# Attention in 64x64 array tiles, softmax sums spread over partitions by transfers, queries transposed by transfers, first batch in two halves

## The chip, the cores and the metric

The kernel runs on one core of one Trainium2 chip. The metric is the device time of one execution in microseconds (us), the median over several executions. A profile of one execution comes with each kernel; its span, from the first to the last instruction, is about 2 us shorter than the time. In the profile PE is TensorE (matmul), PEld its weight loads, DVE VectorE, ACT ScalarE, POOL GpSimd, SP SyncE; "SPq" is SP's instruction queue, which here only issues transfers.

## The reference, cut to what matters

Eight batches, eight heads, 1024 positions, head size 64. Keys and values are projected from 1024 to 64 positions, then ordinary softmax attention follows, then an MLP over all 8192 tokens.

```python
k_proj = einsum('ks,bhsd->bhkd', E, k)                # 64 rows per head
v_proj = einsum('ks,bhsd->bhkd', F, v)
attn   = softmax(q @ k_proj.T / 8)                    # 1024 x 64 per head
x      = (attn @ v_proj)  -> [8192, 512]
out    = (sigmoid(x @ w_gate) * (x @ w_val)) @ w_out  # 512 -> 1536 -> 512
```

Inputs and outputs are float32; the kernel computes its products in bf16.

## The kernel before: the parts that matter

Each batch is split into two MLP blocks of 512 tokens. A block has 12 steps (`mstep`: eight 128x512 matmuls, ACT takes the gate, DVE multiplies) and four output products (`oproj`: 12 matmuls). Pieces of the attention of the next batch are placed between these slots, so PE always has MLP work to do. The attention part, cut (`mm`, `act` and `dve` put a matmul, an ACT and a DVE instruction into the program, `add` one of any engine; `bank` is one of the program's eight tiles into which matmuls write; `tp=` names the tile of the array that a matmul uses):

```python
def qt(r):                # queries of two heads transposed on PE, 128x64 tiles
    ...                   # 16 transposes per r, four r per batch; DVE copies the result
def sc(r):                # scores of two heads, block-diagonal keys, full array
    for hf in range(2):
        mm(bk, bank[bk][:, :], kpBD[:, r, :], qT[:, r, hf * 512 : (hf + 1) * 512], ...)
        act(eT[:, r, hf, :], bank[bk][:, :], ..., func=AF.Exp, scale=SCALE)
def den(): ...            # sums by eight matmuls with a 0/1 matrix, 32 columns each
def rec(c): ...           # reciprocal, a quarter at a time
def split(): ...          # reciprocal as two bf16 parts
def bc(c):                # spread over partitions by a matmul with a 0/1 matrix
    mm(bk, bank[bk][:, :], bsel[:, j, rnd, :], rhl[:, :], ["bsel", "rhl"])
    dve(lambda e: e.tensor_tensor(aT[c % 2][:, :], eT[:, r, hf, :], bank[bk][:, :], ALU.mult), ...)
def xo(c):                # output of two heads, block-diagonal values, full array
    mm(bk, bank[bk][:, :], vpBD[:, r, :], aT[c % 2][:, :], ...)
    act(xT[s][:, r, hf * 512 : (hf + 1) * 512], bank[bk][:, :], ...)
```

At the start, all of K, V and Q of the first batch is loaded, then the weights; the whole attention of the first batch runs before the first MLP step.

The softmax here doesn't subtract the row's maximum and nothing guards it: scores larger than these inputs give would overflow.

## Time and profile before

| | before |
|---|---|
| time, median | 628.68 us (3 runs, 628.39 to 629.42) |
| PE busy, share of the span | 94% |
| period of one batch in steady state | 73.1 us |
| MLP of one batch on PE: 288 matmuls of 0.216 us | 62.2 us |
| attention of one batch on PE | 10.9 us (the difference) |
| first MLP matmul | 43.8 us |

From the profile page of the kernel before: the span, the busy times, then one digit per fortieth of the span for PE's busy share and its granted clock in tenths, and the shares of the chain of waits that ended last.

```profile
span 627.3 us, 8171 instructions
...
PE 589.8 (94%) x3344; PEld 274.7 (44%) x3408; DVE 275.8 (44%) x413; ACT 204.5 (33%) x363; POOL 32.4 (5%) x60
...
PE   2558999999999999999999999999999999999997
...
PEclk9978999999999999999999999999999999999999
...
PE 88%; DMA 6%; POOL 2%; DVE 2%; issue 1%; ACT 1%; DVEq 0%; POOLq 0%
```

From the fourth slice on PE is busy 80% or more and bounds the kernel. Before that it waits. The timeline of PE shows the start (columns: start us, length us, what, how often, and in brackets the idle time before and what ended it).

```profile
12.44 1.92 PE L202 MATMUL pA<-Kb,ET 128*64 128x256 bf16 x16 [6.72 <-DMA Kb<-in_k_dram]
17.56 1.92 PE L202 MATMUL pA<-Vb,FT 128*64 128x256 bf16 x16 [3.21 <-DMA Vb<-in_v_dram]
22.61 1.06 PE L202 MATMUL pA<-ident,Qb 128*64 128x128 bf16 x16 [3.13 <-DMA Qb<-in_q_dram]
...
35.93 1.03 PE L202 MATMUL pA<-rhl,bsel 128*128 128x512 bf16 x2 [4.74 <-DVE rhl L458]
...
43.76 1.02 PE L202 MATMUL pG<-xT,wG 128*128 128x512 bf16 x4
```

The steady state: in the same timeline, one group of query transposes, one pair of score matmuls, one spreading matmul and one output product.

```profile
128.90 0.64 PE L202 MATMUL pA<-ident,Qb 128*64 128x128 bf16 x16
...
132.07 0.59 PE L202 MATMUL pA<-qT,kpBD 128*128 128x512 bf16 x2
...
163.83 0.38 PE L202 MATMUL pA<-rhl,bsel 128*128 128x512 bf16 x1
164.04 0.38 PE L202 MATMUL pA<-aT,vpBD 128*128 128x512 bf16 x1
```

A length is more than the spacing: the two last lines are 0.38 us long and 0.21 us apart. Spacing is what counts.

### The profile page before, as it was taken

To read this page: it belongs to the slowest core of one execution; us is meant where nothing else is said; L and a number is where in the kernel's file an instruction comes from. 1 tells how busy PE (TensorE), PEld (TensorE's weight loads), DVE (VectorE), ACT (ScalarE), POOL (GpSimd) and SP (SyncE) were. 2 spreads that over 40 slices of the span, in tenths; PEclk is the share of its full clock that TensorE was granted. 3 is DMA by queue.
4 is the path that set the end of the run, shared out by engine and by line. 5 is a ranking of instruction groups with operands and counts; after the bars stand their busy time and mean duration, and the time that the engine had idled before them with its cause. 6 is when DMAs were issued, how large, how long until landed. Compare 5 with 4: busy or idle time off the path is not lost.

```text
span 627.3 us, 8171 instructions
## 1 busy us (share of the span) xinstructions
PE 589.8 (94%) x3344; PEld 274.7 (44%) x3408; DVE 275.8 (44%) x413; ACT 204.5 (33%) x363; POOL 32.4 (5%) x60
## 2 busy tenths in 40 slices
PE   2558999999999999999999999999999999999997
PEld 1313444544444444544445444444445444444443
DVE  2162465336543365334653365433653346533332
ACT  1333424232333324333242323333243332422220
POOL 8301000100001000100001000000000000000000
PEclk9978999999999999999999999999999999999999
DMA  9999990652009500375006620000000000000002
GB/s 138 207 207 207 207 175 34 113 106 67 34 35 152 101 34 19 63 138 85 34 34 111 114 62 34 34 18 33 34 24 27 34 18 34 34 34 33 34 33 84
DMA packets 39092, 47.44 MB, mean 76 GB/s; under 512 B 1552, under 2 KB 30736, under 8 KB 39056
## 3 DMA queue, kind: packets, MB, share of 16 engines
q0 software_dynamic: 29840, 30.15, 30.4%
q1 hardware_dynamic: 9216, 16.78, 7.2%
q8 instruction: 26, 0.43, 0.3%
q14 instruction: 10, 0.08, 0.0%
HBM read 60.29 MB, written 16.78 MB: 123 GB/s over the span
## 4 chain that ended last, share of the span: by engine, by line
PE 88%; DMA 6%; POOL 2%; DVE 2%; issue 1%; ACT 1%; DVEq 0%; POOLq 0%
PE pG L202 26%; PE pO L202 25%; PE pV L202 25%; PE pA L202 12%; DMA Qb<-in_q_dram 6%; DVE ost L563 1%; DVE aT L471 1%; ACT sig L206 1%; POOL wG L221 0%; POOL dsel L258 0%; POOL wV L221 0%; POOL Kb L221 0%; POOL Vb L221 0%; POOL bsel L251 0%; POOL Qb L221 0%
## 5 line engine op out<-in xcount | busy, mean ns | idle before, releaser
L536 DVE SCALAR_TENSOR_TENSOR hT<-sig,pV 128x512 bf16<-128x512 f32 x192 | 132.1, 688 | 211.4 <-PE pV L202 207.2
L202 PE MATMUL pG<-xT,wG 128*128 128x512 bf16 x750 | 195.4, 380 | 2.2 <-issue 1.4
L202 PE MATMUL pV<-xT,wV 128*128 128x512 bf16 x746 | 195.7, 380 | 0.8
L206 ACT ACTIVATE sig<-pG 128x512 f32<-128x512 f32 x192 | 114.8, 598 | 246.1 <-PE pG L202 231.7
L202 PE MATMUL pO<-wO,hT 128*128 128x512 bf16 x717 | 166.1, 379 | 2.3 <-issue 1.0
L202 PEld LDWEIGHTS pV<-xT,wV 128*128 128x128 bf16 x768 | 75.4, 98 | 91.2 <-issue 1.1
L202 PEld LDWEIGHTS pG<-xT,wG 128*128 128x128 bf16 x768 | 72.2, 98 | 88.2 <-issue 4.4
L202 PEld LDWEIGHTS pO<-wO,hT 128*128 128x128 bf16 x732 | 70.6, 98 | 85.8 <-DVE ost L563 1.3
L563 DVE TENSOR_SCALAR ost<-pO 128x512 f32<-128x512 f32 x61 | 42.2, 692 | 104.4 <-PE pO L202 104.4
L206 ACT ACTIVATE xT<-pA 128x512 bf16<-128x512 f32 x64 | 38.3, 598 | 68.2 <-PE pA L202 68.0
L206 ACT ACTIVATE eT<-pA 128x512 bf16<-128x512 f32 x64 | 34.7, 596 | 48.5 <-PE pA L202 48.5
L471 DVE TENSOR_TENSOR aT<-eT,pA 128x512 bf16<-128x512 bf16 x64 | 43.5, 681 | 2.1 <-PE pA L202 2.0
L448 DVE RECIPROCAL rden<-pA 128x128 f32<-128x128 f32 x32 | 30.0, 946 | 2.1 <-PE pA L202 2.1
L405 DVE COPY qT<-pA 128x1024 bf16<-128x1024 bf16 x32 | 22.1, 690 | 18.2 <-PE pA L202 18.2
L202 PE MATMUL pA<-rhl,bsel 128*128 128x512 bf16 x58 | 23.0, 400 | 6.2 <-DVE rhl L458 5.0
L202 PE MATMUL pA<-ident,Qb 128*64 128x128 bf16 x512 | 21.5, 229 | 4.3 <-DMA Qb<-in_q_dram 4.0
L202 PE MATMUL pA<-aT,vpBD 128*128 128x512 bf16 x63 | 24.4, 387 | 0.8 <-DVE aT L471 0.7
L202 PEld LDWEIGHTS pA<-ident,Qb 128*64 128x64 bf16 x512 | 16.2, 114 | 18.4 <-issue 11.4
L202 PE MATMUL pA<-qT,kpBD 128*128 128x512 bf16 x63 | 19.1, 384 | 0.8 <-ACT kpBD L206 0.5
L221 POOL DMA_DIRECT2D Kb<-in_k_dram x8 | 7.2, 899 | 217.6 <-PE pA L202 217.6
L202 PE MATMUL pA<-Kb,ET 128*64 128x256 bf16 x128 | 9.4, 294 | 6.7 <-DMA Kb<-in_k_dram 6.7
L202 PE MATMUL pA<-Vb,FT 128*64 128x256 bf16 x128 | 9.2, 292 | 5.5 <-DMA Vb<-in_v_dram 5.5
(53 smaller groups left out, 119.3 us busy)
## 6 DMA issues: line engine op xcount, KB each, us to landing
out_dram<-ost SPq DMA_DIRECT2D x64, 256.0 KB, 2.0
Kb<-in_k_dram POOLq DMA_DIRECT2D x8, 1024.0 KB, 9.8
Vb<-in_v_dram POOLq DMA_DIRECT2D x8, 1024.0 KB, 14.6
Qb<-in_q_dram POOLq DMA_DIRECT2D x8, 1024.0 KB, 13.9
wG<-in_moe_w_gate_dram POOLq DMA_DIRECT2D x3, 512.0 KB, 19.4
wV<-in_moe_w_val_dram POOLq DMA_DIRECT2D x3, 512.0 KB, 21.2
wO<-in_moe_w_out_dram POOLq DMA_DIRECT2D x1, 1536.0 KB, 44.3
Ebf<-in_E_dram POOLq DMA_DIRECT2D x1, 128.0 KB, 2.9
```

The costliest lines, as they stand in the source:

```text
L202: return add("PE", lambda e: e.matmul(o, lhsT, rhs, **kw), r=r, x=[("bank", b)])
L206: return add("ACT", lambda e: e.activation(o, i, func, scale=scale), r=r, w=w, x=x)
L221: add("POOL", lambda e: e.dma_start(o, i), r=r, w=w, dma=sem)
L405: dve(lambda e: e.tensor_copy(qT[:, r, :], ob[:, :]), [], [("qT", r)], b=bk)
L448: lambda e: e.reciprocal(rden[:, cc], bank[bk][:, cc]),
L471: lambda e: e.tensor_tensor(aT[c % 2][:, :], eT[:, r, hf, :], bank[bk][:, :], ALU.mult),
L536: lambda e: e.scalar_tensor_tensor(hT[blk % 2][:, m, :], sg[:, :], 1.0, bank[PV[M % 2]][:, :], ALU.add, ALU.mult,),
L563: lambda e: e.tensor_scalar(o[:, :], bank[pb][:, :], 0.5, None, op0=ALU.mult),
```

## The change

The intent is to take attention work off PE and to start the MLP earlier:

- Scores and outputs use 64x64 tiles of the array, four of which are meant to run at once, in place of block-diagonal operands half filled with zeros.
- Queries are transposed by transfers on SP's queue, not on PE.
- The reciprocals of the softmax sums are spread over 64 partitions by transfers on SP's queue, 16 per batch of 128 KB each, not by matmuls. The product with the reciprocal moves behind the output matmul.
- The first batch is processed in two halves on PE, with the loads reordered, so that the MLP starts with half of it.
- The banks are regrouped: four in turn for the MLP and its outputs, four for attention.

The core of the diff, with cuts marked:

```diff
-            def bc(c):
-                ...
-                mm(bk, bank[bk][:, :], bsel[:, j, rnd, :], rhl[:, :], ["bsel", "rhl"])
-                dve( ... aT[c % 2][:, :], eT[:, r, hf, :], bank[bk][:, :], ALU.mult ... )
+            def one_row(a, n):
+                return bass.AP(a.tensor, a.offset, [list(a.ap[0]), [0, n], list(a.ap[1])])
+
+            def spread():
+                for n in range(8):
+                    for c in range(2):
+                        row = 32 * (n % 4) + 2 * (n // 4) + c
+                        add(
+                            "SP",
+                            lambda e, n=n, c=c, row=row: e.dma_start(
+                                rb[64 * c : 64 * c + 64, n, :],
+                                one_row(rden[row : row + 1, :], 64),
+                            ),
+                            r=[("rden", i) for i in range(4)], w=[("rb", n, c)], dma=f"rb{n}",
+                        )
 ... (the output product: 64x64 tiles, then DVE)
+                            mm(bks[g], bank[bks[g]][64 * c : 64 * c + 64, :],
+                                vpD[kk, 2 * r + c, :], eT[kk, n, :],
+                                VPD + [("eT", n)], tp=(64 * (g ^ c), 64 * c))
+                        dve( ... xT[s][:, r, :, 256 * g : 256 * g + 256] = bank * rb[:, n, :] ... )
 ... (queries)
+        def transpose_q(b):
+            for r in range(NR):
+                add("SP", lambda e, r=r: e.dma_start_transpose(qT[s][:, 2 * r : 2 * r + 2, :]..., Qb[s]...), ...)
 ... (places of the eight attention steps among a batch's 32 slots)
+                spots = (12, 14, 16, 18, 20, 20, 24, 26)      # first batch
+                spots = (3, 6, 10, 14, 18, 18, 25, 29)        # the others: kv, kt, sc, sc, den, spread, xo, xo
```

Each spreading transfer reads one partition of the tile of reciprocals 64 times and writes 64 partitions.

## The prediction

> **What bounds the kernel now.** TensorE. The page's busy table gives PE 94% of the 627.3 us span; the chain that ended last is 88% PE. In steady state one batch takes 73.1 us (output groups at 155.57 and 228.68 us in the timeline), and in such a stretch PE is busy 72.4 of 73.0 us at clock 1.00. A back-to-back 128x512 matmul costs 0.216 us (four in 0.863). The MLP needs 24 x 8 + 8 x 12 = 288 of these per batch, 62.2 us; attention takes the other 10.9 us. Second, the start: the first MLP matmul comes only at 43.8 us (timeline). K, V and Q land at 12.4, 17.5, 22.6 us (5.1 us each), then a serial chain of attention steps follows, with a 4.7 us wait for the split reciprocal and a granted clock of 0.5 in places.
>
> **What changes on PE per batch.** Gone: four groups of query transposes (about 2.9 us together) and eight sum-broadcast matmuls (8 x 0.216 = 1.7). Score and output products go from 16 full matmuls (3.5 us) to 32 in 64x64 tiles, in groups of four. [...] the trace shows only column tiles overlapping (16 projections of 256 columns in about 1.0 us; 8 of the 32-column sums in 0.6 us). If four overlap: 8 x 0.216 plus four joints of 0.2, about 2.5 us. Kept: K/V projections 2.2, K transpose 0.4, sums 0.55. Attention then costs about 5.7 us of PE instead of 10.9, period about 68 us: 7 x 5.2 = 36 us gained, all critical.
>
> **Other engines.** DVE loses four 0.69 us copies and the split; ACT loses eight 0.6 us evictions. Neither was the limit. Four reciprocals (3.8 us) now run together, but an output projection (2.6 us) follows.
>
> **Start.** Loads are reordered: K, half of Q, V, small weight chunks. At 5.1 us per MB, V lands near 18 to 19, and the first weights before 22. The first MLP matmul should start near 24 us, 20 us earlier. The second half-unit costs about 4 us of PE later, and a cold clock and late loads perhaps 4 to 6.
>
> **Sum.** 24 start + 497 MLP + 40 attention (7 x 5.7) + 4 second half + 3 tail + 6 cold clock = 574 span; with the 1 to 2 us between span and time, **576 us** (range 566 to 600). Chances: faster by over 2% 0.87, within 2% 0.04, slower 0.09.
>
> **What shows it.** Period 67 to 69 us between output groups; no transposes on PE after the first batch; a group of eight 64x64 matmuls in 0.5 to 0.7 us; first MLP matmul at 22 to 27 us; PE busy over 95% from there.
>
> **What would break it.** (1) The spreading transfers: 16 of 128 KB per batch, each reading one partition 64 times. [...] Then DVE would wait on these transfers[...]. The placement argues against it, but nothing in this trace shows it. (2) Slow query transposes, holding output transfers behind them on the same queue. (3) 64x64 tiles overlapping only in pairs: period 70 us, time near 590.

The sum's terms: 24 + 497 + 40 + 4 + 3 + 6 = 574 us, and 576 with the time outside the span. That four 64x64 tiles overlap, on which the 40 rests, was supposition, and the joints of 0.2 us an estimate (in the trace of the kernel before the last matmul of a group is 0.38 us long where the spacing is 0.216). So are the 6 us for the clock: in that trace PE is idle from 31.2 to 35.9 us, the granted clock is 0.50 from 34 to 40 us and 0.71 to 0.72 from 49 to 55 us, and the slices below full clock (31 to 43 and 49 to 55 us) fall short of it by about 5 us together. Point (1) under "What would break it" had worked out a time for the spreading transfers and from it the stall of PE. DVE would wait if they were slow, with roughly 14 and 22 us left for them by the program (7 and 11 of a batch's 32 places). The sum has no term for it.

## More of the kernel before

The scores are small, so every softmax sum over 64 terms is close to 64. A kernel that divides by the sum of another row still passes the comparison.

## The result, and the profile after

The changed kernel takes 954.14 us (median of 4 runs, 950.99 to 956.3) against 629.05 us (4 runs) before: a ratio of 1.516, 95% interval 1.511 to 1.522. Ratios here are the mean time of one kernel's fast runs over that of the other's of the same rounds, so not quite the ratio of the medians.

The page of the changed kernel, the same lines as before, and the shares of the chain of waits by line and tile:

```profile
span 950.5 us, 7628 instructions
...
PE 588.6 (62%) x3015; PEld 256.1 (27%) x3072; DVE 248.0 (26%) x376; ACT 174.7 (18%) x315; POOL 30.2 (3%) x43
...
PE   4975510897219973099631995419953299433998
...
PEclk9996855899568995699865998659986599775999
...
PE 35%; DMA 31%; SPq 29%; DVE 4%; issue 1%; POOL 0%; ACT 0%; DVEq 0%; POOLq 0%
PE pF L215 32%; SPq L674 29%; DMA rb<-rden 22%; DMA Qb<-in_q_dram 4%; DMA qT<-Qb 3%; DVE rden L659 2%; PE pA L215 2%; DMA KV<-in_k_dram 1%; DVE xT L701 1%; DVE hT L765 1%; SPq L596 0%; DVE ost L792 0%; POOL KV L233 0%; ACT sig L219 0%; DVEq L102 0%
...
rb<-rden SPq DMA_DIRECT2D x112, 128.0 KB, 15.5
```

PE is no longer the limit. A pattern repeats once per batch: a stretch of nines, then a hole, with the clock falling in it. Over half of the chain, 29% and 22%, is the spreading transfers, `rb<-rden` on line 674. The last line is from the list of transfers: 112 of them (16 for each of seven batches), 15.5 us from issue to landing, several in flight at once.

Who waits for them is in the waits of DVE (first line) and of PE (the rest): engine, line, what it waited for, us in total, times, longest.

```profile
DVE xT L701 <- DMA rb<-rden: 344.0, 53, 9.3
```

```profile
PE pF L215 <- DVE xT L701: 161.6, 14, 16.1
PE pF L215 <- DVE hT L765: 135.6, 6, 22.9
PE pA L215 <- DVE xT L701: 27.1, 4, 9.1
PE pA L215 <- DMA qT<-Qb: 15.6, 3, 10.6
```

DVE waits 344 us for spread reciprocals. PE waits for DVE: 161.6 + 135.6 + 27.1 = 324 us. With the slower clock (about 30 us, see below) this is about what the repaired kernel copies8 gains, 351 us. (That the kernel is also 325 us slower than the one before is chance: the gains of the change lie in between.) A steady batch in the timeline shows how. First SP's queue and DVE:

```profile
332.72 60.02 SPq L674 DMA_DIRECT2D rb<-rden  x16
```

```profile
344.52 0.69 DVE L701 TENSOR_TENSOR xT<-pA,rb 128x512 bf16<-128x512 f32 x1 [0.70 <-DMA rb<-rden]
353.51 0.69 DVE L701 TENSOR_TENSOR xT<-pA,rb 128x512 bf16<-128x512 f32 x1 [8.30 <-DMA rb<-rden]
363.34 0.69 DVE L701 TENSOR_TENSOR xT<-pA,rb 128x512 bf16<-128x512 f32 x1 [9.13 <-DMA rb<-rden]
370.96 0.69 DVE L701 TENSOR_TENSOR xT<-pA,rb 128x512 bf16<-128x512 f32 x1 [6.94 <-DMA rb<-rden]
371.57 0.68 DVE L765 SCALAR_TENSOR_TENSOR hT<-sig,pF 128x512 bf16<-128x512 f32 x1
...
403.38 0.69 DVE L701 TENSOR_TENSOR xT<-pA,rb 128x512 bf16<-128x512 f32 x1 [6.08 <-DMA rb<-rden]
```

and PE in the same stretch:

```profile
311.63 0.63 PE L215 MATMUL pA<-qT,kpD 64*64 64x512 bf16 x8
...
342.96 0.63 PE L215 MATMUL pA<-eT,vpD 64*64 64x512 bf16 x8
...
348.71 1.03 PE L215 MATMUL pF<-xT,wV 128*128 128x512 bf16 x4
372.31 1.89 PE L215 MATMUL pF<-xT,wG 128*128 128x512 bf16 x4 [22.57 <-DVE hT L765]
...
387.50 0.61 PE L215 MATMUL pF<-xT,wG 128*128 128x512 bf16 x1 [5.97 <-DVE xT L701]
404.12 0.61 PE L215 MATMUL pF<-xT,wG 128*128 128x512 bf16 x1 [16.02 <-DVE xT L701]
```

The 16 transfers are issued from 332.72 us and the product that needs the last of them starts at 403.38: 70.7 us for 16 x 131,072 bytes, 29.7 GB/s. Each product needs two transfers, 5.9 to 9.9 us. The MLP's gate product (`hT`) whose matmuls ended before 350 us runs only at 371.57, straight after the last of four waiting attention products, which stand before it in DVE's program; meanwhile PE has no MLP bank that DVE has emptied, and stops. The three idle times add to 44.6 us per batch, and the period is 116.5 us (output products at 312.19 and 428.71 us), where 67 to 69 were predicted. The four matmuls after the longest take 1.89 us where four take 1.03 otherwise, at a granted clock of 0.50: PE is idle from 349.7 us, the granted clock is 1.00 up to 352 us and 0.50 from 353 us, and it stays at 0.50 up to 376 us, some 4 us after PE starts again. PE's busy time is 588.6 us here and 560.4 in q1_pe_again below, which does about 2 us more on PE (the transposes of one batch of queries), so by estimate the slower clock cost about 30 us.

The rest of the picture is as intended: groups of eight 64x64 matmuls take 0.63 us, and the first MLP matmul comes at 25.76 us.

### The profile page after: what moved, and what is told of

Its sections match the earlier page's. It is cut to its first block, busy times and chain, and to the rows that moved or that the text cites. A ratio compares the mean times of both kernels' runs of the same rounds, so it can differ in the third digit from the quotient of the medians.

```text
span 950.5 us, 7628 instructions
## 1 busy us (share of the span) xinstructions
PE 588.6 (62%) x3015; PEld 256.1 (27%) x3072; DVE 248.0 (26%) x376; ACT 174.7 (18%) x315; POOL 30.2 (3%) x43
## 4 chain that ended last, share of the span: by engine, by line
PE 35%; DMA 31%; SPq 29%; DVE 4%; issue 1%; POOL 0%; ACT 0%; DVEq 0%; POOLq 0%
PE pF L215 32%; SPq L674 29%; DMA rb<-rden 22%; DMA Qb<-in_q_dram 4%; DMA qT<-Qb 3%; DVE rden L659 2%; PE pA L215 2%; DMA KV<-in_k_dram 1%; DVE xT L701 1%; DVE hT L765 1%; SPq L596 0%; DVE ost L792 0%; POOL KV L233 0%; ACT sig L219 0%; DVEq L102 0%
## 5 line engine op out<-in xcount | busy, mean ns | idle before, releaser
L215 PE MATMUL pF<-xT,wG 128*128 128x512 bf16 x744 | 212.9, 403 | 299.4 <-DVE xT L701 161.6
L219 ACT ACTIVATE sig<-pF 128x512 f32<-128x512 f32 x192 | 114.5, 597 | 682.0 <-PE pF L215 677.4
L215 PE MATMUL pF<-xT,wV 128*128 128x512 bf16 x752 | 211.9, 403 | 2.1 <-ACT rb L219 1.2
L765 DVE SCALAR_TENSOR_TENSOR hT<-sig,pF 128x512 bf16<-128x512 f32 x192 | 131.7, 686 | 215.9 <-PE pF L215 183.4
L215 PEld LDWEIGHTS pF<-xT,wG 128*128 128x128 bf16 x768 | 75.3, 102 | 408.1 <-DVE xT L701 169.0
L215 PE MATMUL pF<-wO,hT 128*128 128x512 bf16 x751 | 175.9, 383 | 1.3 <-issue 0.5
L701 DVE TENSOR_TENSOR xT<-pA,rb 128x512 bf16<-128x512 f32 x56 | 38.7, 691 | 356.7 <-DMA rb<-rden 344.0
L215 PEld LDWEIGHTS pF<-xT,wV 128*128 128x128 bf16 x768 | 78.8, 103 | 100.5 <-issue 16.2
L215 PEld LDWEIGHTS pF<-wO,hT 128*128 128x128 bf16 x768 | 73.6, 99 | 94.9 <-issue 10.7
L792 DVE TENSOR_SCALAR ost<-pF 128x512 f32<-128x512 f32 x64 | 43.7, 683 | 110.1 <-PE pF L215 110.1
L215 PE MATMUL pA<-eT,vpD 64*64 64x512 bf16 (+1 forms) x136 | 13.1, 428 | 27.1 <-DVE xT L701 27.1
L215 PE MATMUL pA<-qT,kpD 64*64 64x512 bf16 (+1 forms) x136 | 10.6, 377 | 16.1 <-DMA qT<-Qb 15.6
L219 ACT ACTIVATE kp<-pA 128x256 bf16<-128x256 f32 x8 | 3.1, 383 | 35.9 <-PE pA L215 35.9
## 6 DMA issues: line engine op xcount, KB each, us to landing
rb<-rden SPq DMA_DIRECT2D x112, 128.0 KB, 15.5
KV<-in_k_dram POOLq DMA_DIRECT2D x8, 1024.0 KB, 15.6
```

The costliest lines, as they stand in the source:

```text
L215: return add("PE", lambda e: e.matmul(o, lhsT, rhs, **kw), r=r, x=[("bank", b)])
L219: return add("ACT", lambda e: e.activation(o, i, func, scale=scale), r=r, w=w, x=x)
L701: lambda e, r=r, g=g, n=n, bk=bks[g]: e.tensor_tensor(xT[s][:, r, :, 256 * g : 256 * g + 256], bank[bk][:, :].rearrange("p (f c) -> p f c" ...
L765: lambda e: e.scalar_tensor_tensor(hT[blk % 2][:, m, :], sg[:, :], 1.0, bank[pv][:, :], ALU.add, ALU.mult,),
L792: lambda e: e.tensor_scalar(o[:, :], bank[pb][:, :], 0.5, None, op0=ALU.mult),
```

## The experiments

Theory SOURCE: a spreading transfer is slow because all its reads go to one partition. "Port", here and in the expectations, is only a name for a set of partitions whose reads share one limit; that there are such sets was a supposition, which near4, copies4, near4b and alternate test. Rivals: ISSUE (each instruction costs SP 4.76 us, whatever it reads), DESTINATION (64 partitions, or 2 MB, limit it), and for the loss as a whole: the query transposes on the same queue, or the mere place of the transfers in the program.

Times of single looks are of one run, whose state is unknown; those with an interval are of fast runs. In each single look the output matmuls average 0.38 us, as in the changed kernel, so none of them is slow in the way of the one slow run below (0.83 us). The kernel before took 628.4 to 631.2 us on the same chips.

### rows64: the same transfers, 64 partitions read

```diff
-                                one_row(rden[row : row + 1, :], 64),
+                                rden[64 * c : 64 * c + 64, :],
```

> Wrong result on purpose: each of the 16 spreading transfers per batch reads 64 different partitions (rows 0 to 63 or 64 to 127 of the reciprocals) in place of one partition 64 times; bytes, number of rows, destination, queue and place in the program stay. Theory SOURCE (the one partition read by all 16 engines limits a transfer to about 29.7 GB/s, 4.4 us for 128 KB): a transfer falls under 1.2 us, 16 of them under 18 us in place of 70, the period of a batch from 116.5 to 68 to 72 us, the time to 590 to 620 us. Rival ISSUE (SP's 4.76 us per transfer is the cost of issuing or of making 64 rows of descriptors) and rival DESTINATION (64 destination partitions, or the 2 MB as such, limit it): no change, 16 transfers 70 us, time 945 to 960 us.

Measured: 596.30 us. SP's queue needs 10.4 us for the 16 issues, 0.6 us each, and a transfer lands 2.3 us after issue. The period is 67.9 us (output products at 194.03 and 261.92 us). ISSUE and DESTINATION fall: instructions, bytes, rows and destination are the same. The result passes the comparison although the rows are the wrong ones.

### rotate: one partition per transfer, the next copy for the next transfer

The kernel's 0/1 matrix writes eight equal copies of each sum, four partitions apart.

```diff
-                        row = 32 * (n % 4) + 2 * (n // 4) + c
+                        row = 32 * (n % 4) + 2 * (n // 4) + c + 4 * ((2 * n + c) % 8)
```

> Right result: the kernel holds eight equal copies of each row of reciprocals, four partitions apart. Each transfer still reads one partition 64 times, but transfer after transfer takes the next copy[...]. Theory SOURCE in its strict form (all 16 engines work on one transfer at a time, in order, so one port is busy at a time): hardly a change, 16 transfers 60 to 70 us, time 900 to 955 us. If the engines run ahead into the next transfers and spread over ports: 16 transfers 20 to 45 us, time 640 to 800 us. Rivals ISSUE and DESTINATION: no change at all, 945 to 960 us.

Measured: 725.31 us, result right; 16 transfers take about 38 us (issued from 182.44, last product at 220.41), and DVE's waits for them fall from 344 to 121.8 us. The edit leaves each single transfer as it was, so consecutive transfers do overlap when each reads another copy: 38 us in place of 70.7. The strict form of SOURCE, one transfer at a time, was wrong.

### copies8: all eight copies read by each transfer

```diff
-                return bass.AP(a.tensor, a.offset, [list(a.ap[0]), [0, n], list(a.ap[1])])
+                p = list(a.ap[0])
+                return bass.AP(a.tensor, a.offset, [[4 * p[0], 8], [0, n // 8], list(a.ap[1])])
```

> Right result: each transfer reads all eight equal copies of its row (eight partitions, four apart[...]), eight times each, in place of one copy 64 times. Bytes and destination stay[...]. Theory SOURCE: 16 transfers take 10 to 22 us in place of 70, period 68 to 73 us, time 590 to 625 us, faster than the kernel before. Rivals ISSUE and DESTINATION: unchanged, 945 to 960 us.

Measured: 603.13 us (4 runs, 602.49 to 604.70), ratio to before 0.957, interval 0.955 to 0.959, result right. SP's queue in a steady batch, and what PE still waits for:

```profile
231.37 10.83 SPq L675 DMA_DIRECT2D rb<-rden  x16
```

```profile
PE pA L215 <- DMA qT<-Qb: 18.4, 4, 10.9
...
PE pF L215 <- DVE xT L702: 6.2, 2, 3.3
```

60.0 us of issue have become 10.8; the waits of 324 us on DVE are 6.2 us. This small edit, which changes no instruction on PE, DVE or ACT, is worth 954 - 603 = 351 us.

### pe_bcast: the sums spread by TensorE again

Cut: the transfers are replaced by the split into two bf16 parts, eight matmuls of 32 rows in four row tiles, and eight ACT evictions.

```diff
-                spread,
-                lambda: xo(0),
+                (split after den)
+                lambda: bc(0),      # four matmuls, tp=(32 * j, 0), lhsT = bsel4[jj, r2], rhs = rhl4[jj]; four ACT copies to rb
+                lambda: bc(1),
+                lambda: xo(0),
-                spots = (3, 6, 10, 14, 18, 18, 25, 29)
+                spots = (3, 6, 10, 14, 18, 21, 23, 25, 29)
```

> One part of the change undone: the reciprocals are spread over partitions by TensorE again (split into two bf16 parts, eight matmuls of 32 rows in four row tiles, eight ACT evictions of 0.6 us per batch), no spreading transfers. The 64x64 tiles, the query transposes by transfers and the halved first batch stay. If the spreading transfers are the whole loss: no DVE wait of over 1 us on them, period 68 to 70 us, first MLP matmul still near 25.5 us, time 585 to 610 us with the 12 to 16 us of transpose waits in the first batch left in. If the transposes or the output transfers behind them cost as much: above 640 us.

Measured: 605.28 us (4 runs), ratio 0.961, interval 0.959 to 0.963; period 69.1 us (196.93 to 266.02), 1.2 us more than copies8. So it is the spreading that made the change a loss: with it undone and the transposing transfers kept, the kernel beats the one before. Once the source is right, transfers and matmuls are nearly equal here.

### near4 and copies4: port or partition

Both read four partitions sixteen times each, with the same rows of the destination and the same bytes: near4 four neighbours, copies4 four copies four apart.

```diff
 near4:   +  [[1 * p[0], 4], [0, n // 4], list(a.ap[1])]
 copies4: +  [[4 * p[0], 4], [0, n // 4], list(a.ap[1])]
```

> Wrong rows on purpose for three quarters of the reads (all sums are near 64, so the comparison may still pass): each transfer reads four neighbouring partitions sixteen times each[...] If the limit is the PORT: still 4.2 to 4.6 us per transfer, 16 of them in 65 to 75 us, time 930 to 960 us. If the limit is the single PARTITION (or repeated reads of one row): a quarter, 16 transfers in 16 to 25 us, time 590 to 640 us.

> Right result, the counterpart of near4: four copies of the right row, four partitions apart[...], sixteen times each[...]. PORT: about 1.1 to 1.3 us per transfer, 16 in 17 to 24 us, time 600 to 640 us. PARTITION: the same as near4.

Measured: near4 828.36 us, 16 transfers in 52 us (298.50 to 350.58 us); copies4 608.43 us, result right, 16 in 23 us (235.12 to 257.77). copies4 met PORT. near4 met neither number, and the fault was in its design. It took its four partitions to share one port, but its rows started at 0 to 3 of a group of 32, so three in four of its transfers reached across a multiple of four. The first eight, starting at 0 and 1, took 34 us; the last eight, starting at 2 and 3 and all across the edge, 18 us.

How busy the 16 transfer engines are does not show this limit. In copies4 they are 27% busy at 103 GB/s (all transfers, 237 to 252 us), in the changed kernel 88% busy at 31 GB/s (335 to 380 us).

### near4b: near4 mended

```diff
-                        row = 32 * (n % 4) + 2 * (n // 4) + c
+                        row = 32 * (n % 4)
```

> near4 mended. In near4 the four neighbours began at rows 0 to 3 of a group of 32, so most transfers reached over the edge of four partitions[...]; its first eight transfers[...] still took 34 us, the last eight, half across the edge, 18 us. Here all transfers start at row 0 of their group: partitions 0 to 3 (or 32 to 35, 64 to 67, 96 to 99)[...] (wrong rows on purpose). PORT: back to 4.2 to 4.6 us per transfer, 16 in 65 to 72 us, time 930 to 960 us, although four partitions are read in place of one. PARTITION: 16 in 17 to 25 us as in copies4, time 600 to 640 us.

Measured: 1032.82 us. DVE in a steady batch:

```profile
240.01 0.69 DVE L702 TENSOR_TENSOR xT<-pA,rb 128x512 bf16<-128x512 f32 x1 [1.16 <-PE pF L215]
249.96 0.69 DVE L702 TENSOR_TENSOR xT<-pA,rb 128x512 bf16<-128x512 f32 x1 [9.26 <-DMA rb<-rden]
260.28 0.69 DVE L702 TENSOR_TENSOR xT<-pA,rb 128x512 bf16<-128x512 f32 x1 [9.63 <-DMA rb<-rden]
```

About 10 us for two transfers, 82 us for 16 (227.72 to 309.85 us), 25.5 GB/s. Four neighbours (partitions 0 to 3, 32 to 35, 64 to 67 or 96 to 99) are no faster than one partition; four partitions four apart take 23 us. So these neighbours share one limit: PORT stands and PARTITION falls. That this is slower than the single partition (70.7 us) was not expected. In the changed kernel some products come sooner (5.9 to 7.6 us after the one before, the others 9.0 to 9.9); here no product does. near4b also keeps fewer transfer engines busy (23% of 16, 245 to 283 us, against 88%). Why it is slower is open.

How far a port reaches beyond four partitions was not tested by a run of its own. The order in the changed kernel speaks for the groups at 0 and 32 sharing one, and those at 64 and 96 another. Its source goes through partitions 0, 1, 32, 33, then 64, 65, 96, 97, then 2, 3, 34, 35, then 66, 67, 98, 99, with about three transfers in flight (15.5 us to land, one issued every 4.76). Each product has another group of four as its source, yet the products do not come alike: after the first they follow at 9.0, 9.8, 7.6, 9.9, 5.9, 9.9 and 6.8 us, and the sooner ones are the second after each move across partition 64.

### alternate: the same 16 transfers in another order

```diff
-                for n in range(8):
-                    for c in range(2):
+                for a, b2 in ((0, 2), (1, 3), (4, 6), (5, 7)):
+                    for n, c in ((a, 0), (b2, 0), (a, 1), (b2, 1)):
```

> The changed kernel with the same 16 one-partition transfers, in another order[...]. PORT, with engines running a few transfers ahead as in rotate: 16 transfers 36 to 50 us, time 760 to 850 us. If transfers do not overlap: 70 us and 945 to 960 us.

Measured: 767.94 us, result right; 44.6 us for 16 (279.95 to 324.50 us), 47 GB/s. The source now goes through 0, 64, 1, 65, 32, 96, 33, 97, and so on: transfers from below partition 64 and from above it overlap, within the 36 to 50 us expected. In the changed kernel four transfers from below are followed by four from above, and 16 take 70.7 us. So in these runs all 16 rows act as two ports, one below and one above partition 64.

### early: the transfers as they are, twelve places earlier

```diff
-                spots = (3, 6, 10, 14, 18, 18, 25, 29)
+                spots = (0, 1, 2, 4, 6, 6, 25, 29)
```

> The changed kernel with its transfers as they are, but in batches 2 to 7 the sums and the transfers start 12 places (about 26 us) earlier, the products where they were. If only the place were wrong: period near 68 us, time 610 to 640 us. PORT: the transfers still need 70 us, more than a batch's 68 us of PE work, and hold SP's queue with the output transfers behind them: period 88 to 105 us, time 780 to 880 us.

Measured: 915.46 us, period 108.8 us (276.81 to 385.62): hardly better, and above the expected range. The waits of DVE and of PE:

```profile
DVE ost L792 <- DMA out_dram<-ost: 258.5, 6, 46.3
```

```profile
PE pF L215 <- DVE ost L792: 236.7, 6, 42.6
```

The waits on spread reciprocals are down to 58.6 us, but a new wait took their place. The spreading transfers hold SP's queue for 60 us, the output transfers stand behind them, the four output buffers fill, and DVE waits for those. The expectation had named this queue but under-counted it. So earlier places did not mend it while the output transfers share the queue; early places with the outputs on another queue were not tried.

### q1_pe and q1_pe_again: what is left after copies8

copies8 waits 18.4 us for the first query transposes, which run beside the bulk of the loads: in the chain of the changed kernel two of the first four took 12.2 and 16.6 us, against a median of 3.2 us from issue to landing. For the second batch alone, PE transposes again (the edit of copies8, a parameter and a dependency are left out):

```diff
+        load_q(1)
         load_k(1)
         load_v(1)
-        load_q(1)
-                spots = (12, 14, 16, 18, 20, 20, 24, 26)
+                spots = (12, 13, 14, 15, 17, 17, 23, 25)
-                put(turn_at, lambda: transpose_q(1))
+                for i, hf, R in ((11, 0, 0), (12, 1, 0), (13, 0, 1), (14, 1, 1)):
+                    put(i, lambda hf=hf, R=R: half_unit(hf, att, 1)[0](R))
```

> copies8, and for the second batch alone the queries are transposed on TensorE (its Q loaded before its K and V, its later steps a few places earlier), because in copies8 PE waits 18.4 us for these transfers while loads fill the engines. Theory: that wait and the 6.2 us of waits after it, with the cold clock behind them, are what keeps copies8 at 603 instead of the 576 predicted: 576 to 588 us, no PE wait on transposes. Rival (the rest is lost elsewhere, for example in the steady batches or the tail): 596 us or more.

Measured: three runs of 584.4 to 587.0 us, ratio 0.930, interval 0.927 to 0.933. The profiled run took 1497.12 us and is slow: its MLP matmuls average 0.83 us where 0.38 is usual, though the granted clock is recorded as 1.00. It explains nothing about the kernel, so the same kernel was run again:

> The same kernel as q1_pe, whose profiled execution took 1497 us with every matmul slow, while its three others took 584.4 to 587.0 us. If that was a state of the chip and not of the kernel: all runs 583 to 589 us, profile with a period of 67.9 us and no PE wait on transposes over 1 us. If it belongs to the kernel: some runs near 1497 us again.

Measured: 584.82 us (5 runs, 584.20 to 587.22), ratio 0.930, interval 0.928 to 0.932. The page and the chain of this run:

```profile
span 582.3 us, 7749 instructions
...
PE 560.4 (96%) x3104; PEld 252.1 (43%) x3104; DVE 246.4 (42%) x378; ACT 176.0 (30%) x317; POOL 30.3 (5%) x43
...
PE   2799997999999999999999999999999999999997
...
PE 92%; DMA 4%; DVE 1%; ACT 1%; SPq 1%; issue 1%; DVEq 0%; POOLq 0%
```

No wait on transposes is left, and the period is 67.9 us (182.25 to 250.13). This is the best version, 7% faster than the kernel before. The edit bundles three things, the transposes, the load order and the earlier places, which were not tried apart.

### all_q_pe: all queries transposed on TensorE

```diff
-                put(26 if b == 0 else turn_at, lambda b=b: transpose_q(b + 2))
+            if b > 0 and b + 1 < B:
+                for i, hf, R in ((1, 0, 0), (2, 0, 1), (4, 1, 0), (8, 1, 1)):
+                    put(i, lambda b=b, hf=hf, R=R: half_unit(hf, att, (b + 1) % 2)[0](R))
```

> q1_pe with the queries of all batches transposed on TensorE, no transposing transfers: four groups of eight 128x128 transposes and four evictions of 0.7 to 1.0 us per batch. The prediction put the worth of the transfers at about 2.9 us of PE per batch; the new groups of eight take about 0.9 us for two in the trace (16 transposes 0.9 us) plus joints, 2.2 us per batch. Theory: period 70 us in place of 67.9, time 12 to 16 us above q1_pe. If the transfers cost as much as they save (by holding up output transfers): same as q1_pe within 3 us.

Measured: 595.72 us (4 runs, 595.00 to 597.92), ratio 0.947, interval 0.944 to 0.949; period 69.7 us (188.47 to 258.14). That is about 10 us above q1_pe's fast runs of the same rounds, slightly less than the 12 to 16 expected, and 1.8 us per period. So the transposing transfers do pay in the steady state, after the bulk of the loads.

## Why the prediction was wrong, point by point

- **What bounds the kernel before, and PE's new work per batch: right.** Predicted period about 68 us; with the spreading repaired it is 67.9 us in rows64, copies8 and q1_pe_again. The 64x64 groups took 0.63 us, predicted 0.5 to 0.7: four tiles do overlap (if only pairs did, eight should take about as long as four full matmuls, 1.03 us).
- **The start: right.** First MLP matmul at 25.76 us, predicted 22 to 27, and 43.76 before. The halved first batch with its reordered loads brings the MLP forward by 18 us, before the cost of the second half.
- **"The placement argues against it, but nothing in this trace shows it": this is the step that failed.** The prediction named the spreading transfers and DVE's wait for them, and then set them aside because of the places that the program gives them, 14 and 22 us before the uses. The sum therefore had no term for them. Measured, the transfers take 70.7 us and PE stands idle 44.6 us in a steady batch. Repairing the source alone gives back 351 of the 378 us between 954 and the predicted 576. That a program places a use 14 us after its source is no evidence that the source takes under 14 us.
- **The danger had no measured size.** The time that the prediction gave the transfers rested on nothing in the trace of the kernel before. Measured, 16 of them take 70.7 us in the order of the change and 44.6 us in that of alternate.
- **"Four reciprocals ... an output projection follows": right; DVE was not loaded.** Its 248 us of work is less than before. But "neither was the limit" speaks of load only: with 26% of the span busy, DVE still set the pace, as a gate product stood behind attention products whose operand was late (344 us of waits).
- **Breaker (2), slow transposes: true only at the start.** 15.6 us of PE waits in the changed kernel, all beside the bulk loads, none worth naming in the steady state. Removing them, with the load order and places, took copies8 from 603 to 585 us.
- **What remains: 585 against 576,** 9 us. The start is 2 us later than in the sum; the rest of it was not taken apart.

## What to carry to other kernels

Before moving a broadcast from TensorE to transfers, count the partitions from which each transfer reads and see how far apart they are, not only the bytes: here 2 MB read from one partition per transfer held SP's queue for 60 us, from four neighbours for 55 (near4b), from eight partitions four apart for 11. Where a matmul with a 0/1 matrix makes the result, as here, the same matmul can write copies on other partitions, and the access pattern can read them all. And a hazard that has been costed belongs in the sum with its cost; the schedule is not a measurement.

## What else the runs showed

- Rates of the spreading transfers, 2,097,152 bytes from the first issue to the last product: 29.7 GB/s in the changed kernel (probably with some overlap, where some products come sooner), 25.5 in near4b, 47 in alternate, 93 in copies4 (22.65 us).
- In the changed kernel a transposing transfer of 256 KB landed in 3.2 us (median of 28), ordinary outputs of 256 KB in 2.4; beside bulk loads, two took 12.2 and 16.6 us. The outputs go elsewhere (to DRAM), so the two are not compared like for like.
- The output products have two row tiles write different halves of the partitions of one bank. Their groups of eight took the same 0.63 us as the score products, which keep the row tiles in different banks (eight one after another would need 8 x 0.216 = 1.7 us); the results are right.
- q1_pe's slow run took 1497 us throughout with matmuls of 0.83 us at a recorded clock of 1.00, one of nine runs of that kernel. Its cause is not shown.
